# Talking-heads attention and a seven-product MLP on one core: one weight product for all four batches, with the conversion's stores and loads placed anew

## The chip, the cores and the metric

The kernel runs on one core of a Trainium2 chip. The metric is the device time of one execution in microseconds. Three runs of the kernel before gave 1107.64, 1112.34 and 1112.71 us.

## What is computed

Queries, keys, values and mixing weights come in float32, the two MLP weights in float64 (two 32-bit words to a number); inside, each matmul operand is a float32r number, for most operands with a second one that holds the rest. With 4 batches, 12 heads, 448 positions and head size 64:

```python
scores = np.matmul(q, k.transpose(0, 1, 3, 2)) / np.sqrt(64)
scores = np.einsum('bhij,hg->bgij', scores, w_pre)          # mix heads
attn = softmax(scores)
attn = np.einsum('bhij,hg->bgij', attn, w_post)             # mix heads again
x = np.matmul(attn, v).transpose(0, 2, 1, 3).reshape(1792, 768)
h = x @ w_in                                                # 768 x 2048
return (h / (1 + np.exp(-h))) @ w_out                       # 2048 x 768
```

## The kernel before

**Attention.** The scores of 16 tiles (4 batches of 4) are worked on in 180 groups of 10 query rows times 12 heads. For each group TensorE (PE) mixes the heads (`pp`, L317), VectorE (DVE) takes the maximum (`nm`, L323), ScalarE (ACT) the exponential (`e`, L328), GpSimd (POOL) scales the second mixing matrix (`wr`, L336), and PE mixes again (`pa`, L343). In between, the scores of the next tile are made (`pqk`, L277), copied to one of three buffers `st` by ACT (L282) and sent to the group layout `g` by a DMA (L283); the values `po` (L292) of the tile before go through `xb` to `x_dram` (L305). All DMAs are issued by SyncE (SP), in the order in which the program is written: a DMA that waits for its data or its buffer holds up all those behind it.

**Conversion.** `convert` (L38) turns the float64 weights into float32 sums of blocks, in 48 jobs of two parts. A part is a load `cw` (L47, 256 KB), four DVE operations (L82, L88, L89, L63), one of ACT (L86) and a POOL product `cg` (L69); after the second part POOL adds seven block sums (L71 to L74) and a store (L57, 448 KB) puts them into `wi_dram` or `wo_dram`. It is a generator of three pieces to a part; 38 jobs run beside the attention, a part in about two groups, the other 10 in the MLP, three pieces in two steps. A load is issued three parts ahead; with one `cg` buffer the store is issued in the piece right after POOL's last sum.

**MLP.** Each of two units (u = 0, 1) holds two batches. A product of a 2 x 2 block matrix is made from seven block products (`ORDER`, L465), first x by w_in ("i"), then the result by w_out ("o"). A step is one output block of one block product: 9 matmuls of 128x448 in "i" (8 steps to a block product), 24 in "o" (3 steps). The order is u = 0 "i", u = 0 "o", u = 1 "i", u = 1 "o" (L486). For every step the weights are loaded (`wl`, L501), rounded by ACT (`wh`, L513) and the rest is taken by POOL or DVE (`wl`, L525); thus each weight block is loaded and split twice, once for each unit. The operands `op` of a block product are halved by ACT (L549) and DVE (L551) one block product ahead, in one of two sets; `differ` (L553) and `second` (L559, with `t`) make the combined blocks with DVE and POOL. `evacuate` (L718) takes PSUM out after each step. x is read back from `x_dram` in chunks (`load_x`, L468) and added by POOL for unit 0 and by DVE for unit 1.

Of the kernel before, what the change touches and what calls it, by code (L numbers as in the profile page):

```python
# [8 lines left out]
F32 = mybir.dt.float32  # L9
# [28 lines left out]
def convert(nc, pool, ebias, jobs, bufs):  # L38

    parts = [(n, i) for n in range(len(jobs)) for i in (1, 0)]  # L40
    loaded, held = [], []

    def load(k):
        if k < len(parts):
            n, i = parts[k]
            ws = pool.tile([128, 2, 256], I32, name="cw", tag="cw", bufs=4)
            nc.sync.dma_start(out=ws, in_=jobs[n][0][:, i])  # L47
            loaded.append(ws.rearrange("p q (w t) -> p q w t", t=2))
# [5 lines left out]
    def store(most=0):  # L54
        while len(held) > most:
            dst, g = held.pop(0)
            nc.sync.dma_start(out=dst, in_=g)  # L57

    def finish(k, pair, e):
# [6 lines left out]
        if i:  # L66
            finish.g = pool.tile([128, 7, 128], F32, name="cg", tag="cg", bufs=bufs)
        g = finish.g
        nc.gpsimd.tensor_mul(out=g[:, 0:2] if i else g[:, 2:4], in0=m, in1=e.bitcast(F32))  # L69
        if not i:  # L70
            nc.gpsimd.tensor_add(out=g[:, 4], in0=g[:, 0], in1=g[:, 1])  # L71
            nc.gpsimd.tensor_add(
                out=g[:, 5:7], in0=g[:, 0:5:4], in1=g[:, 2:3].to_broadcast([128, 2, 128]))
            nc.gpsimd.tensor_add(out=g[:, 0], in0=g[:, 6], in1=g[:, 3])  # L74
            held.append((jobs[n][1], g))

    before = None
    for k in range(len(parts)):
        pair = loaded.pop(0)
        hi = pair[:, :, :, 1]  # L80
        e = pool.tile([128, 2, 128], I32, name="ce", tag="ce", bufs=2)
# [8 lines left out]
        store(bufs - 1)  # L90
        load(k + 3)
        before = k, pair, e
# [9 lines left out]
def talking_heads_then_silu_mlp(  # L102
# [41 lines left out]
    wi_dram = [dram.tile([128, 7, HC, 128], F32, name=f"wi_dram{f}") for f in range(HF)]  # L144
    wo_dram = [dram.tile([128, 7, HF, 128], F32, name=f"wo_dram{c}") for c in range(HC)]
# [213 lines left out]
    jobs = [(wi_src[:, f, c], wi_dram[f][:, :, c, :]) for f in range(HF) for c in range(HC)]  # L359
    jobs += [(wo_src[:, c, f], wo_dram[c][:, :, f, :]) for c in range(HC) for f in range(HF)]  # L360
    NA = 38
    conv = convert(nc, c_p, ebias, jobs[:NA], 1)
# [56 lines left out]
    for i in range(0, n_last, 10):  # L419
        lighter |= set(sorted(range(i, min(i + 10, n_last)), key=lambda i: weight[i - 1] if i else 0.0)[:10])  # L420
# [45 lines left out]
    xs, gr, ops, box = {}, {}, {}, {}  # L466

    def load_x(u, ls, lag, add):  # L468

        chunks = [(j, l, c) for l in ls for j in range(2) for c in range(HC)]  # L470
        xr = []
        for n in range(len(chunks) + lag):
            if n >= lag:
                r = xr[n - lag]
                add.tensor_add(out=xs[chunks[n - lag]], in0=r[:, 0], in1=r[:, 1])
            if n < len(chunks):
                j, l, c = chunks[n]
                xr.append(box["xr"].tile([128, 2, T], F32, name="xr", tag="xr"))
                for o in range(2):
                    nc.sync.dma_start(  # L480
                        out=xr[n][o * D:(o + 1) * D],
# [4 lines left out]
    steps = [(u, kind, k, a) for u in range(NU) for kind, n in (("i", HF), ("o", HC)) for k in range(7) for a in range(n)]  # L486
    parts, part_of = [], []
    for u, kind, m, a in steps:
        part_of.append(len(parts))
        if kind == "i":  # L490
            parts.append((wi_dram[a][:, ORDER[m]], HC))
        else:
            parts += [(wo_dram[a][:, ORDER[m], h:h + 4], 4) for h in range(0, HF, 4)]
    part_of.append(len(parts))
    raws, ready = {}, {}

    def load_to(i):
        for j in range(load_to.n, min(i, len(parts))):
            w, n = parts[j]
            raws[j] = box["w"].tile([128, 4, 128], F32R, name="wl", tag="wl", bufs=5)  # L500
            nc.sync.dma_start(out=raw(raws[j][:, :n]), in_=w)  # L501
            load_to.n = j + 1

    load_to.n = 0

    turn = {part_of[s] + d for s, x in enumerate(steps) if x[1:] == ("o", 0, 0) for d in range(4)}

    def high_to(i):
        for j in range(high_to.n, min(i, len(parts))):
            high_to.n = j + 1  # L510
            n = parts[j][1]
            wh = box["w"].tile([128, 4, 128], F32R, name="wh", tag="wh", bufs=5)
            nc.scalar.copy(out=wh[:, :n], in_=raw(raws[j][:, :n]))  # L513
            ready[j] = wh, raws.pop(j)

    high_to.n = 0

    def ready_to(i):
        high_to(i)
        for j in range(ready_to.n, min(i, len(parts))):  # L520
            ready_to.n = j + 1
            n = parts[j][1]
            wh, wl = ready[j]
# [3 lines left out]
    ready_to.n = 0  # L527

    def operand(kind, k):

        if kind == "i":
            return [ops[3 * (k % 2) + c] for c in range(HC)]
        return [ops[8 * (1 - k % 2) + c] for c in range(HF)]

    def product(s, p):

        u, kind, k, a = steps[s]
        xs_ = operand(kind, k)
        w = [(ready[j][0][:, c], ready[j][1][:, c]) for j in range(part_of[s], part_of[s + 1]) for c in range(parts[j][1])]
        for n, (x, (wh, wl)) in enumerate(zip(xs_, w)):  # L540
            nc.tensor.matmul(p[:, :T], lhsT=wh, rhs=x[:, 0], start=(n == 0), stop=False)  # L541
            nc.tensor.matmul(p[:, :T], lhsT=wh, rhs=x[:, 1], start=False, stop=False)  # L542
            nc.tensor.matmul(p[:, :T], lhsT=wl, rhs=x[:, 0], start=False, stop=(n == len(xs_) - 1))  # L543
        for j in range(part_of[s], part_of[s + 1]):
            del ready[j]
# [13 lines left out]
    def second(blocks, c, dst):  # L559

        t = box["t"].tile([128, T], F32, name="t2", tag="t2", bufs=4)
        nc.vector.tensor_sub(out=t, in0=blocks[1, 1, c], in1=blocks[0, 0, c])  # L562
        yield
        nc.scalar.copy(out=dst[:, 0], in_=t)
        yield
        nc.gpsimd.tensor_sub(out=blocks[1, 0, c], in0=t, in1=blocks[1, 0, c])  # L566
# [3 lines left out]
    first_step = {(u, kind, k): s for s, (u, kind, k, a) in reversed(list(enumerate(steps)))}  # L570
# [8 lines left out]
    for u in range(NU):  # L579
        for kind, n, blocks in (("i", HF, xs), ("o", HC, gr)):  # L580
            for m in range(7):
                s = first_step[u, kind, m]
                nk = HC if kind == "i" else HF
                if m == 2:
                    todo = [lambda b=blocks, c=c, kind=kind: second(b, c, operand(kind, 2)[c]) for c in range(nk)]
                else:
                    todo = [lambda b=blocks, c=c, kind=kind, m=m: halve(b[(*SOURCE[m], c)], operand(kind, m)[c]) for c in range(nk)]
                if m == 0 and kind == "i":
                    if u:
                        put_at(s - HC, HC, todo)  # L590
                elif m == 0:
                    put_at(s - 2 * HF, 2 * HF - 2, todo)
                else:
                    lag = 3 if (kind, m) == ("i", 2) else 0
                    put_at(s - n + lag, n - lag - (kind == "i"), todo)
# [234 lines left out]
```

## Time and profile before

| | |
|---|---|
| median of three runs | 1112.34 us |
| profiled execution: its time / its span | 1114.52 / 1112.8 us |
| PE, PEld busy | 985.9 us (89%), 792.2 us (71%) |
| DVE, ACT, POOL busy | 778.8 us (70%), 645.0 us (58%), 562.3 us (51%) |
| mean granted TensorE clock | 0.955 |
| DMA queue of SP | 216068 packets, 174.11 MB |

Busy times are unions over an engine's instructions; matmuls overlap in the records, so a busy PE need not be PE at its best pace. Times inside the program are counted from the start of the span. The attention fills the first 623 us, the MLP the rest.

### The profile page before, as it was taken

How to read it: one execution, taken by the hardware profiler on the slowest of the kernel's cores; microseconds unless marked ns; L12 is line 12 of the kernel's file. 1: busy time of each engine (PE TensorE's matmuls, PEld its weight loads, DVE VectorE, ACT ScalarE, POOL GpSimd, SP SyncE). 2: the span in 40 equal slices, each digit the busy share in tenths (PEclk: the TensorE clock that was granted, in tenths of full speed). 3: DMA queues.
4: the chain of work that ended last, by engine and by line, in shares of the span. 5: the costliest groups of instructions: out<-in, count | busy, mean ns of one | idle time of the engine just before them, and what ended most of it. 6: DMA issues, size and time to landing. Idle time of an engine off the chain costs nothing. (4 is left out here: it accounts for less than half of the span.)

```text
span 1112.8 us, 18086 instructions
## 1 busy us (share of the span) xinstructions
PE 985.9 (89%) x5448; PEld 792.2 (71%) x5448; DVE 778.8 (70%) x1751; ACT 645.0 (58%) x1562; POOL 562.3 (51%) x674
## 2 busy tenths in 40 slices
PE   5888999798899988898998878888899999988998
PEld 3456666565676666566777767777699889977897
DVE  2567768766787777488766389887996264869742
ACT  4666666665677766577775444564355453652543
POOL 0354334543344633245414387746965395559752
PEclk8889999988999989899999889999999999999999
DMA  6556756756667666567535756645475433333343
GB/s 169 160 172 173 202 169 195 199 156 174 186 178 215 190 175 172 165 172 199 163 111 146 183 159 193 206 126 146 129 206 145 133 102 106 107 106 84 109 123 96
DMA packets 216164, 175.25 MB, mean 157 GB/s; under 512 B 79524, under 2 KB 205316, under 8 KB 216068
## 3 DMA queue, kind: packets, MB, share of 16 engines
q1 hardware_dynamic: 216068, 174.11, 56.4%
q8 instruction: 44, 0.72, 0.3%
q14 instruction: 52, 0.43, 0.1%
HBM read 96.77 MB, written 38.58 MB: 122 GB/s over the span
## 5 line engine op out<-in xcount | busy, mean ns | idle before, releaser
L543 PE MATMUL ph<-op,wl 128*128 128x448 f32 x672 | 255.1, 380 | 37.6 <-POOL wl L525 29.7
L525 POOL TENSOR_TENSOR wl<-wl,wh 128x384 fp32r<-128x384 f32 (+1 forms) x165 | 211.4, 1292 | 122.5 <-ACT wh L513 115.4
L541 PE MATMUL ph<-op,wh 128*128 128x448 f32 x672 | 253.9, 378 | 2.0 <-ACT wh L513 1.6
L542 PE MATMUL ph<-op,wh 128*128 128x448 f32 x672 | 252.1, 375 | 2.9 <-DVE op L567 2.7
L336 POOL TENSOR_SCALAR wr<-wpost,r 120x120 f32<-120x120 f32 x180 | 85.2, 474 | 308.6 <-DVE r L334 242.5
L343 PE MATMUL pa<-wr,e 120*112 120x120 f32 x1440 | 194.1, 280 | 9.0 <-DVE r L333 7.5
L343 PEld LDWEIGHTS pa<-wr,e 120*112 120x112 f32 x1440 | 168.9, 184 | 36.9 <-issue 20.0
L317 PE MATMUL pp<-g,wpre 120*120 120x448 f32 x360 | 174.9, 570 | 12.1 <-ACT e L328 8.0
L292 PE MATMUL po<-at,v 112*128 112x220 f32 (+1 forms) x768 | 172.5, 352 | 2.6 <-ACT st L282 2.3
L323 DVE TENSOR_REDUCE nm<-pp 120x1 f32<-120x448 f32 x180 | 111.2, 618 | 87.9 <-PE pp L317 86.8
L543 PEld LDWEIGHTS ph<-op,wl 128*128 128x128 f32 x672 | 130.3, 194 | 59.5 <-POOL wl L525 38.3
L513 ACT CAST wh<-wl 128x384 fp32r<-128x384 f32 (+1 forms) x196 | 107.6, 556 | 106.1 <-DMA wl<-wo_dram 54.5
L292 PEld LDWEIGHTS po<-at,v 112*128 112x128 f32 x768 | 115.0, 196 | 71.1 <-issue 53.2
L328 ACT ACTIVATE e<-pp,nm 120x448 f32<-120x448 f32 x180 | 114.7, 637 | 61.0 <-DVE nm L323 60.5
L542 PEld LDWEIGHTS ph<-op,wh 128*128 128x128 f32 x672 | 130.3, 194 | 15.8 <-DVE op L567 4.3
L352 ACT CAST at<-pa 112x480 fp32r<-112x480 f32 x180 | 102.8, 571 | 66.4 <-PE pa L343 65.9
L541 PEld LDWEIGHTS ph<-op,wh 128*128 128x128 f32 x672 | 130.3, 194 | 13.7 <-ACT wh L513 2.2
L282 ACT COPY st<-pqk 110x448 f32<-110x448 f32 (+1 forms) x192 | 98.0, 542 | 69.9 <-DMA g<-st 66.3
L355 DVE TENSOR_TENSOR at<-pa,at 112x480 fp32r<-112x480 f32 x180 | 116.4, 646 | 4.9 <-ACT at L352 4.9
L551 DVE TENSOR_TENSOR op<-g,op 128x448 fp32r<-128x448 f32 x96 | 84.9, 922 | 42.1 <-ACT op L549 42.0
L277 PE MATMUL pqk<-kh,qh 64*110 64x448 f32 (+1 forms) x192 | 65.9, 463 | 47.2 <-ACT st L282 19.0
L69 POOL TENSOR_TENSOR cg<-cw,ce 128x256 f32<-128x256 f32 x96 | 76.4, 796 | 59.2 <-DVE cw L63 20.9
(82 smaller groups left out, 1394.8 us busy)
## 6 DMA issues: line engine op xcount, KB each, us to landing
g<-st SPq DMA_DIRECT2D x144, 192.5 KB
wl<-wi_dram SPq DMA_DIRECT2D x112, 192.0 KB
wl<-wo_dram SPq DMA_DIRECT2D x84, 256.0 KB
cw<-in_moe_w_in SPq DMA_DIRECT2D x48, 256.0 KB
cw<-in_moe_w_out SPq DMA_DIRECT2D x48, 256.0 KB
wi_dram<-cg SPq DMA_DIRECT2D x24, 448.0 KB
wo_dram<-cg SPq DMA_DIRECT2D x24, 448.0 KB
xr<-x_dram SPq DMA_DIRECT2D x48, 224.0 KB
```

The costliest lines, as they stand in the source:

```text
L292: nc.tensor.matmul(po[:, :2 * m].rearrange("p (w t) -> p w t", w=2), lhsT=vs[b, h][:, j].rearrange("p a d -> p (a d)"), rhs=ats[n][:, j, h ...
L317: nc.tensor.matmul(self.p[:GP, :S], lhsT=wpre.rearrange("p i g -> p (i g)"), rhs=gs[self.n][:, self.slot, :], start=True, stop=True)
L323: nc.vector.tensor_reduce(out=self.nm, in_=self.p[:GP, :S], axis=AX.X, op=ALU.max, negate=True)
L328: nc.scalar.activation(out=self.e, in_=self.p[:GP, :S], func=AF.Exp, bias=self.nm, scale=1.0, accum_out=self.s)
L343: nc.tensor.matmul(self.pa[:JT, j * GP:(j + 1) * GP], lhsT=self.e[:, j * JT:(j + 1) * JT], rhs=self.wr, start=True, stop=True)
L352: nc.scalar.copy(out=self.hi, in_=self.src)
L355: nc.vector.tensor_sub(out=self.lo, in0=self.src, in1=raw(self.hi))
L513: nc.scalar.copy(out=wh[:, :n], in_=raw(raws[j][:, :n]))
L525: eng.tensor_sub(out=wl[:, :n], in0=raw(wl[:, :n]), in1=raw(wh[:, :n]))
L541: nc.tensor.matmul(p[:, :T], lhsT=wh, rhs=x[:, 0], start=(n == 0), stop=False)
L542: nc.tensor.matmul(p[:, :T], lhsT=wh, rhs=x[:, 1], start=False, stop=False)
L543: nc.tensor.matmul(p[:, :T], lhsT=wl, rhs=x[:, 0], start=False, stop=(n == len(xs_) - 1))
```

## The change

- The MLP's steps are ordered by block product first and unit second (`steps`): all seven block products of "i" for u = 0 and u = 1 in turn, then those of "o". The weights come in parts of four 128-column blocks, six to a block product and 84 in all, each loaded, rounded and split once (`load_part`, `ready_part`); POOL makes every difference. `load_at` and `high_at` say in which step a part is loaded and made ready; seven buffers (WB) hold the parts.
- Each unit has one set of operands `ops[u]`, rewritten while the other unit's product of the same number runs. `differ` and `second` of both units therefore fall into neighbouring steps.
- Unit 1's x is read during the first block product of "i" and added by POOL.
- In `convert` the store of a job is issued one part after its sums (`store()` at odd k), the load of part k+1 at the start of part k, with three `cw` and two `cg` buffers; the exponent part is made inside `cg`. 34 jobs (NA) run beside the attention, in 8 of every 10 groups; 14 in the MLP, one piece in a step.
- `oT` has two buffers for three, `t` three for four; seven `wl` loads for three are issued in the last tile, and two plus four weight parts are made ready before the MLP.

```diff
     for k in range(len(parts)):
+        if k > 1:
+            load(k + 1)
         pair = loaded.pop(0)
         hi = pair[:, :, :, 1]
-        e = pool.tile([128, 2, 128], I32, name="ce", tag="ce", bufs=2)
+        if k % 2 == 0:
+            g = pool.tile([128, 7, 128], F32, name="cg", tag="cg", bufs=2)
+        else:
+            store()
+        half = g[:, 2 * (k % 2):2 * (k % 2) + 2]
+        e = half.bitcast(I32)
...
-        store(bufs - 1)
-        load(k + 3)
...
-    NA = 38
-    conv = convert(nc, c_p, ebias, jobs[:NA], 1)
+    NA = 34
+    conv = convert(nc, c_p, ebias, jobs[:NA])
...
-        lighter |= set(sorted(range(i, min(i + 10, n_last)), key=lambda i: weight[i - 1] if i else 0.0)[:10])
+        lighter |= set(sorted(range(i, min(i + 10, n_last)), key=lambda i: weight[i - 1] if i else 0.0)[:8])
...
-    steps = [(u, kind, k, a) for u in range(NU) for kind, n in (("i", HF), ("o", HC)) for k in range(7) for a in range(n)]
+    steps = [(kind, k, u, a) for kind, n in (("i", HF), ("o", HC)) for k in range(7) for u in range(NU) for a in range(n)]
+    NP = HF * HC // 4
+    parts = [(src, ORDER[k], p) for src in (wi_dram, wo_dram) for k in range(7) for p in range(NP)]
...
+    WB = NP + 1
+    for j in range(WB, len(parts)):
...
+        s = step_of[kind0, m0, NU - 1, (4 * p0 + 3) // n] + 1
+        s = max(s, step_of[kind, m, 0, 0] - (10 if kind == "i" or m == 0 else 3))
+        load_at[s].append(j)
+        high_at[s + (3 if s < step_of["o", 0, 0, 0] - 2 else 1)].append(j)
...
-            eng = nc.vector if j % 2 and (2 <= j < 7 * HF or j in turn) else nc.gpsimd
-            eng.tensor_sub(out=wl[:, :n], in0=raw(wl[:, :n]), in1=raw(wh[:, :n]))
+        nc.gpsimd.tensor_sub(out=wl, in0=raw(wl), in1=raw(wh))
...
+                if kind == "i" and u and not m:
+                    put_at(s - n + 3, n - 3, todo)
+                elif m or u:
+                    put_at(s - n, n - (kind == "i"), todo)
+                elif kind == "o":
+                    put_at(s - HF, HF - 1, todo)
                 if m == 1:
-                    lag = n if kind == "i" else 0
-                    put_at(s - n + lag, n // 2 if lag else n, [lambda b=blocks, c=c: differ(b, c) for c in range(nk)])
+                    put_at(s, n, [lambda b=blocks, c=c, u=u: differ(b[u], c) for c in range(nk)])
...
         if s > 2:
             next(conv, None)
-            if s % 2:
-                next(conv, None)
```

SP in the attention, around a store of the conversion (`cg`), before; `st` to `g` are the scores, `xb` the values:

```order
L283 DMA g<-st 10x11x448 x2
L57 DMA wi_dram_72<-cg 896x1x128
L47 DMA cw<-in_moe_w_in 128x2x256
L305 DMA x_dram_67<-xb 128x2x110
L283 DMA g<-st 10x11x448 x2
```

The same place after the change:

```order
L284 DMA g<-st 10x11x448 x2
L47 DMA cw<-in_moe_w_in 128x2x256
L206 DMA kn<-in_k 112x4x64 x2
L306 DMA x_dram_67<-xb 128x2x110
L243 DMA qn<-in_q 120x6x64
L47 DMA cw<-in_moe_w_in 128x2x256
L57 DMA wi_dram<-cg 896x1x128
```

The store went from just ahead of the scores' next DMAs to behind the load of the following part.

SP at the start of the MLP after the change; `xr` are chunks of x for unit 1, `cw` the MLP's first conversion loads:

```order
L306 DMA x_dram_70<-xb 128x2x110 x7
L481 DMA xr_7540<-x_dram_69 64x2x448 x2
L481 DMA xr_7541<-x_dram_69 64x2x448 x2
L481 DMA xr_7540<-x_dram_69 64x2x448 x2
L481 DMA xr_7541<-x_dram_69 64x2x448 x2
L47 DMA cw<-in_moe_w_out 128x2x256 x3
```

DVE there, after the change (`op` are unit 1's first operands, L86 and L92, L93 the conversion):

```order
L539 TENSOR_TENSOR op_8041<-x_8035,op_8041 128x448
L86 TENSOR_SCALAR cg<-cw 128x256
L539 TENSOR_TENSOR op_8042<-x_8036,op_8042 128x448
L92 SCALAR_TENSOR_TENSOR cg<-cw,cg 128x256
L93 TENSOR_SCALAR cw<-cw 128x256
L539 TENSOR_TENSOR op_8043<-x_8037,op_8043 128x448
```

Ahead of the three `cw` loads SP now has four chunks on two buffers, and a conversion operation stands between the first and the second of unit 1's operands.

DVE in the second product, block products 1 and 2, before (unit 1; `g` the blocks, L555 `differ`, L562 and L567 `second`):

```order
L555 TENSOR_TENSOR g_8213<-g_8221,g_8213 128x448
L562 TENSOR_TENSOR t_11720<-g_8230,g_8206 128x448
L562 TENSOR_TENSOR t_11723<-g_8231,g_8207 128x448
L567 TENSOR_TENSOR op_8198<-t_11720,op_8198 128x448
```

The same place after the change (L543 `differ` of unit 1, L550 and L555 `second` of unit 0):

```order
L543 TENSOR_TENSOR g_8083<-g_8075,g_8083 128x448
L550 TENSOR_TENSOR t_10458<-g_8060,g_8052 128x448
L550 TENSOR_TENSOR t_10463<-g_8061,g_8053 128x448
L550 TENSOR_TENSOR t_10465<-g_8062,g_8054 128x448
L555 TENSOR_TENSOR op_7537<-t_10458,op_7537 128x448
L732 TENSOR_TENSOR oT<-ph,x_8035 128x448
L555 TENSOR_TENSOR op_7538<-t_10463,op_7538 128x448
```

One unit's `differ` and the other's `second` now stand in the same three steps.

## Rows read from the trace of the kernel before

**Rows 1.** Windows: start:end, length; busy us (count) PE PEld DVE ACT POOL; clock, DMA, GB/s.

```profile
45.00:603.00 558.00, 497.64 (x3093) 365.41 (x3093) 406.10 (x1209) 374.95 (x1010) 233.44 (x387) 0.96 0.63 175
...
623.30:756.70 133.40, 111.00 (x488) 95.81 (x488) 107.93 (x196) 67.47 (x143) 84.38 (x90) 0.94 0.63 178
756.70:878.30 121.60, 111.74 (x546) 100.33 (x544) 96.39 (x100) 55.02 (x105) 84.49 (x57) 0.97 0.56 151
878.30:985.20 106.90, 105.86 (x515) 95.07 (x513) 62.61 (x90) 60.60 (x126) 66.65 (x61) 1.00 0.41 113
985.20:1106.50 121.30, 112.12 (x543) 101.30 (x543) 79.72 (x86) 53.05 (x102) 80.11 (x55) 0.96 0.37 102
940.60:970.35 29.75, 29.75 (x145) 27.03 (x144) 21.48 (x32) 19.28 (x40) 15.55 (x16) 1.00 0.38 106
```

**Rows 2.** Tile ph, what its engine sat idle for: us, times.

```profile
  POOL wl L525: 68.0, 44
...
  DVE wl L525: 18.0, 12
```

**Rows 3.** Groups of DVE by line, 623 to 745 us: count, busy us, mean ns, idle before.

```profile
L88 DVE SCALAR_TENSOR_TENSOR ce<-cw,ce 128x256 int32<-128x256 int32 x20 | 13.9, 696 | 5.3 <-ACT ce L86 5.3
L525 DVE TENSOR_TENSOR wl<-wl,wh 128x384 fp32r<-128x384 f32 x23 | 13.7, 594 | 3.5 <-ACT wh L513 3.5
L89 DVE TENSOR_SCALAR cw<-cw 128x256 int32<-128x256 int32 x20 | 13.1, 653 | 0.7
...
L82 DVE TENSOR_SCALAR ce<-cw 128x256 int32<-128x256 int32 x20 | 8.4, 419 | 5.7 <-DMA cw<-in_moe_w_out 5.7
L63 DVE SCALAR_TENSOR_TENSOR cw<-cw 128x256 f32<-128x256 uint32 x20 | 8.3, 415 | 0.0
...
L745 DVE TENSOR_TENSOR g<-g,ph 128x448 f32<-128x448 f32 x8 | 4.9, 616 | 1.1 <-PE ph L543 1.0
```

**Rows 4.** Timeline of the MLP's first steps: start us, us, what [idle before <- releaser].

```profile
625.10 2.54 SPq L480 DMA_DIRECT2D xr<-x_dram  x4
...
627.80 1.50 SPq L47 DMA_DIRECT2D cw<-in_moe_w_out  x3
...
629.82 1.13 POOL L475 TENSOR_TENSOR x<-xr 128x448 f32<-128x448 f32 x1 [3.07 <-DMA xr<-x_dram]
...
632.89 0.45 DVE L82 TENSOR_SCALAR ce<-cw 128x256 int32<-128x256 int32 x1 [5.66 <-DMA cw<-in_moe_w_out]
...
633.86 0.74 PE L543 MATMUL ph<-op,wl 128*128 128x448 f32 x1 [4.46 <-DVE wl L525]
```

**Rows 5.** Timeline of DVE, second product of unit 1.

```profile
990.73 1.16 DVE L551 TENSOR_TENSOR op<-g,op 128x448 fp32r<-128x448 f32 x2 [2.48 <-ACT op L549]
...
992.35 0.61 DVE L551 TENSOR_TENSOR op<-g,op 128x448 fp32r<-128x448 f32 x1
...
1006.10 3.33 DVE L555 TENSOR_TENSOR g<-g,g 128x448 f32<-128x448 f32 x2
...
1031.05 3.06 DVE L567 TENSOR_TENSOR op<-t,op 128x448 fp32r<-128x448 f32 x2
```

**Rows 6.** Timeline of POOL, the same stretch.

```profile
985.28 1.29 POOL L525 TENSOR_TENSOR wl<-wl,wh 128x512 fp32r<-128x512 f32 x1 [2.32 <-ACT wh L513]
...
1008.91 1.54 POOL L557 TENSOR_TENSOR g<-g,g 128x448 f32<-128x448 f32 x1
1010.41 3.31 POOL L525 TENSOR_TENSOR wl<-wl,wh 128x512 fp32r<-128x512 f32 x2
```

**Rows 7.** Waits of SP's queue, 45 to 590 us: us in total, times, longest.

```profile
SPq L283 <- ACT st L282: 69.9, 51, 5.0
SPq L57 <- POOL wr L336: 62.7, 26, 6.5
```

**Rows 8.** Waits of the engines, 45 to 590 us.

```profile
ACT st L282 <- DMA g<-st: 57.5, 36, 4.2
...
PE pqk L277 <- ACT st L282: 19.0, 13, 3.9
```

**Rows 9.** Groups of DVE by line, 45 to 590 us.

```profile
L323 DVE TENSOR_REDUCE nm<-pp 120x1 f32<-120x448 f32 x166 | 102.5, 618 | 74.6 <-PE pp L317 73.6
```

**Rows 10.** The chain that ended last, 884 to 889 us.

```profile
884.92 3.51 DMA wl<-wi_dram
```

More of the change, by code (lines that the diff above doesn't have):

```diff
@@ L52, in convert, with store, finish @@
     yield
-    def store(most=0):
-        while len(held) > most:
-            dst, g = held.pop(0)
+    def store():
+        while made:
+            dst, g = made.pop(0)
             nc.sync.dma_start(out=dst, in_=g)
-    def finish(k, pair, e):
+    def finish(k, pair, g, e):
         n, i = parts[k]
@@ L65, in finish @@
             op0=ALU.mult, op1=ALU.add if i else ALU.subtract)
[L66 to L69, printed above, removed]
+        nc.gpsimd.tensor_mul(out=e, in0=m, in1=e)
         if not i:
@@ L487, in talking_heads_then_silu_mlp @@
[L487 to L494, printed above, removed]
-    raws, ready = {}, {}
[L497 to L502, printed above, removed]
@@ new lines, in talking_heads_then_silu_mlp, with load_part, ready_part @@
+    high_at[3].append(NP)
+    def load_part(j):
+        src, k, p = parts[j]
+        if src is wo_dram:
+            for _ in conv:
+                pass
+        raws[j] = box["w"].tile([128, 4, 128], F32R, name="wl", tag="wl", bufs=WB)
+        nc.sync.dma_start(out=raw(raws[j]), in_=src[:, k, 4 * p:4 * p + 4])
+    def ready_part(j):
+        wl = raws.pop(j)
+        wh = box["w"].tile([128, 4, 128], F32R, name="wh", tag="wh", bufs=WB)
+        nc.scalar.copy(out=wh, in_=raw(wl))
+        nc.gpsimd.tensor_sub(out=wl, in0=raw(wl), in1=raw(wh))
+        ready[j] = wh, wl
@@ L541, in product @@
+    def product(s, p):
+        kind, k, u, a = steps[s]
+        nk = HC if kind == "i" else HF
+        for n in range(nk):
+            wh, wl = (x[:, (a * nk + n) % 4] for x in ready[part_of(kind, k, a * nk + n)])
+            x = ops[u][n]
             nc.tensor.matmul(p[:, :T], lhsT=wh, rhs=x[:, 0], start=(n == 0), stop=False)
             nc.tensor.matmul(p[:, :T], lhsT=wh, rhs=x[:, 1], start=False, stop=False)
-            nc.tensor.matmul(p[:, :T], lhsT=wl, rhs=x[:, 0], start=False, stop=(n == len(xs_) - 1))
@@ L544, in product @@
-        for j in range(part_of[s], part_of[s + 1]):
-            del ready[j]
+            nc.tensor.matmul(p[:, :T], lhsT=wl, rhs=x[:, 0], start=False, stop=(n == nk - 1))
     def halve(src, dst):
@@ L788, in talking_heads_then_silu_mlp @@
         each = -(-len(todo) // rounds)
-        for _ in range(rounds):
+        last = a == (HF if kind == "i" else HC) - 1
+        while todo or rounds > 0 or last and active:
+            rounds -= 1
             active.extend(todo[:each])
```

187 lines of the change are left out of this document (85 added, 102 removed).

## The prediction

> **What bounds the kernel now.** I read the windows by stage first: in each row the reader should compare PE's count and busy time with the length. The quiet row at the end of the group gives PE's pace where nothing holds it: 16 steps of 9 matmuls in 29.75 us, so 0.2066 us a matmul [rows 1]. At that pace unit 0's first product from step 2 on (54 steps, 486 matmuls) needs 100.4 us and took 133.4, a loss of 33.0. Unit 1's (504 matmuls, 104.1 us) took 106.9, a loss of 2.8. The two second products (504 each) took 121.6 and 121.3, a loss of 17.5 and 17.2, with the output transposes in it, which stay. Next I asked what PE stood idle for at the tile of the MLP's results: 68.0 us in 44 waits for weight remainders made by POOL, 18.0 in 12 for those made by DVE [rows 2]. So the MLP is held by the splitting of weights, most of all where the conversion shares the engines. In the attention PE was busy 497.6 of 558.0 us at a mean clock of 0.96 [rows 1]; 19.0 us of its idle time ended with ACT's copy of scores, and ACT itself waited 57.5 us for earlier scores' DMAs [rows 8]. SP, which issues them in order, stood 62.7 us in 26 waits at the conversion's store, whose sums POOL had not made [rows 7].
>
> **First product: 18 us gained.** The change halves the weight work: 196 loads, roundings and differences become 84, of 512 columns where most had 384, and DVE makes none. What takes over is DVE's total. Before, in 8 steps (14.9 us) of unit 0, DVE had 4 conversion parts of 0.696 + 0.653 + 0.419 + 0.415 = 2.18 us, 8 evacuations of 0.616, 4 weight differences of 0.594 and 3 operand halves of about 0.7 [rows 3]: 8.7 + 4.9 + 2.4 + 2.1 = 18.1, or 3.2 too much, which is why unit 0 lost and unit 1, with no conversion, hardly did. After it, 16 steps (29.75 us) hold 5.3 parts, 16 evacuations and 6 halves: 11.6 + 9.9 + 4.2 = 25.7, which fits, for block products 3 and 4. Block product 1 is the exception: beside evacuations and conversion it has 3 halves, both units' `differ` (6) and unit 0's `second` (6). At 0.61 us where POOL is quiet and 1.67 where POOL runs beside it (3.33 for two) [rows 5], about 1.0 on the mean, that is 11.6 + 9.9 + 15 = 36.5, 7 too much. Four PSUM banks let PE run some steps ahead, so I charge 7 us for it, with block product 2, which only just fits, in that.
>
> The start has a wait of its own. In the present kernel two chunks of x are issued from 625.10 on, the first is added at 629.82; the conversion's loads go out at 627.80, DVE's first conversion operation waits until 632.89, and PE loses 4.46 us behind it [rows 4]. After the change SP has four chunks ahead of those loads, on two buffers, so the third waits for the first to be added. By these rows: first add done 7.6 us after the start of step 2 (630.95 less 623.3), third chunk then out, loads out near 10.3, landed near 15.4. DVE's conversion operation stands before the second operand of unit 1, and ACT's conversion step before the third. PE wants them in step 8, 6 steps or 11.2 us in, and gets them near 17. So 5 to 6 us, and about 2 for the lower clock after it, my estimate from unit 0's mean of 0.94 where the quiet row has 1.00 [rows 1]: 7.5. It takes the place of the present 4.46 and what followed. With 3 for the rest, the loss is 7.5 + 7 + 3 = 17.5 against 33.0 + 2.8 = 35.8. Bounds: 8 us gained if block product 1 costs all the DVE excess twice (both units), 28 if the banks hide it.
>
> **Second product: 8 us gained.** With weights off the path, the work behind `differ` and `second` decides. Now: one unit's chain on DVE ran from 990.73 to 1034.1, 43.4 us [rows 5], for 32 operations on two operands in SBUF and 3 evacuations on DVE, and 28 on POOL (8, 8 and 12 weight differences). DVE alone takes 0.61 [rows 5], POOL alone 1.29 for 512 columns; with both running, one of each takes 1.5 (1008.91 to 1010.41) [rows 6] to 1.67. At 1.55 the sum is 28 x 1.55 + 7 x 0.6 = 47.6, so the measured chain is 0.91 of it. Its last operand was wanted 6 steps of 4.96 us and 4.3 more after 985.2, at 1019.3: 14.8 late, the bulk of 17.2. Both units together: 29.6. After: both units' `differ` and `second` follow on each other. From the first step of block product 1 there are 56 such operations and 9 evacuations on DVE, and 16 + 16 + 7 on POOL: (39 x 1.55 + 26 x 0.6) x 0.91 = 69.2. The last is wanted 9 steps and 4.3 us on, at 48.9: 20.3 late, against 29.6, so 9, and I take 8, since the single operand set can start nothing early. The weight parts have 10 us from load to use (two steps) for 3.5 us of load [rows 10], ACT's rounding and POOL's 1.3 to 1.7 [rows 6], and are late only with the chain. Unit 1's 12 additions of x leave DVE for POOL in the first product, already counted.
>
> **A rule that speaks against this.** Two-operand additions on DVE slow from 0.61 to 1.67 us when POOL runs [rows 5]. The Trainium skill (GPSIMD Engine Reference, Key points) says that GpSimd shares its SBUF interfaces with VectorE and contends with DVE instructions that have two SBUF inputs; the trace agrees. Taken strictly, as turns without overlap, a pair would cost the sum of the two alone, which is the third rival below.
>
> **Attention: 10 us gained.** Four jobs leave, but DVE and POOL are not full there. What counts is SP: the store moves behind the next part's load, so POOL's sums are long made, and the scores' DMAs no longer queue behind it. I take half of PE's 19.0 us [rows 8], as ACT also waits for scores with no store in front. Upper bound: all 19.0 and part of the clock, whose 0.96 over 558 us is 22 us: 25. Lower bound 0, since stores and loads still share the DMA engines. A weight part in the last tile is 256 KB instead of 192, and seven are issued together: 0 to 2 us, within the rounding.
>
> **Sum.** 18 + 8 + 10 = 36 us against the profiled execution's 1114.5; its span is 1112.8, and it stands 2.2 above the median of 1112.3. From the median: **1076 us**.
>
> **Rivals.** First, SP gives more: all PE waits for score copies go (25), block product 1 hides in the banks (24): 1112 - 25 - 24 - 8 = 1055. For it: the 62.7 us [rows 7]; against: ACT's waits also where only scores were issued.
>
> Second, the same sum is lost again: DVE's excess spreads over the first product (108 of 133 us are DVE's already [rows 1]) and the waits only change their name: 1108 to 1112. Against it: unit 1 without conversion loses 2.8.
>
> Third, DVE and POOL take strict turns in the second product: 32 pairs at 0.61 + 1.13 (1.29 for 448 of 512 columns), 7 at 0.61 + 1.29 and 26 x 0.6 make 84.6, or 36 late instead of 20: 1076 + 16 = 1092. Against it: pairs at 1.5 [rows 6].
>
> Fourth, **slower**: a conversion load is now issued one part ahead, not three, and DVE's first operation on it stands in DVE's queue before `nm` of a following group. Two groups take 2 x 545 / 166 = 6.6 us [rows 9], a load 3.5 [rows 10] to 5.1 [rows 4] and SP's own delay. It decides if loads land 7.1 us or more after their part began: at 0.55 us late on each of 66 parts the 36 us are gone, at 1 us it is 1076 + 66 = 1142. Against it: DVE's idle time there hides some, and 3.5 leaves 3 us.
>
> **Chances.** Forecast 0.54, first rival 0.20, second 0.06, third 0.14, fourth 0.06. The range takes the first rival whole and the third with 12 more for its bounds: 1050 to 1104; outside are the second, the fourth, and some of the tails. About 0.5% (5.6 us) is what a measurement here can tell from no change: faster 0.88, same 0.06, slower 0.06.
>
> **What would show it.** Right: 84 splits, no weight difference on DVE; PE's idle time for POOL's weights below 25 us; one stall of 5 us or so near step 8; stalls at block products 1 and 2 of "o" with `second` as releaser, some 20 us; SP's waits at the store near zero. Wrong: a first conversion operation that waits for `cw` in most parts of the attention, or evacuations as releaser through all of the first product.

## The result, and the profile after

The changed kernel takes **1081.73 us** (median of 4 runs, 1077.76 to 1085.65) where the kernel before took 1112.53 on the same chip (4 runs, 1107.64 to 1117.17): a ratio of 0.9724, interval 0.9668 to 0.9779. The forecast was 1076, within 1050 to 1104. A run more than 1.5% above the fastest of its kernel is left out of medians and ratios; that is one run, 1073.96 us of the kernel of four moves below. The profiled execution took 1082.58 us, its span is 1080.9 (before 1114.5 and 1112.8).

For the comparison both spans are cut at three events: the first weight load (`wl`) in the last attention tile, the first matmul of step 2 of the MLP, and the first matmul of the second product. Windows of the kernel after (columns as in [rows 1]):

```profile
45.00:579.70 534.70, 488.27 (x3083) 359.72 (x3080) 392.95 (x1173) 369.56 (x999) 216.76 (x367) 0.98 0.63 175
579.70:610.00 30.30, 19.98 (x122) 17.89 (x121) 9.74 (x31) 10.94 (x34) 16.45 (x16) 0.89 0.77 209
610.00:839.40 229.40, 211.87 (x993) 189.12 (x993) 173.74 (x284) 100.82 (x198) 134.82 (x137) 0.96 0.46 133
839.40:1074.60 235.20, 222.99 (x1095) 200.90 (x1094) 144.25 (x179) 86.71 (x170) 100.93 (x71) 0.96 0.22 61
```

In the kernel before the first weight load is at 603.1, step 2 at 623.4; its products are those of [rows 1], the two units added.

| stretch | before | after | difference | forecast |
|---|---|---|---|---|
| attention, up to the first weight load | 603.1 | 579.7 | -23.4 | -10 |
| hand-over, from there to step 2 | 20.3 | 30.3 | +10.0 | 0 (priced 0 to 2) |
| first products | 240.3 | 229.4 | -10.9 | -18 |
| second products | 242.9 | 235.2 | -7.7 | -8 |
| last transposes and stores | 6.3 | 6.3 | 0 | 0 |
| sum | | | -32.0 | -36 |

So the sum is close, but its parts are not: the attention gave more than twice what was forecast, the hand-over took 10 us back, and the first product gave 7 less. The MLP, for which the weights are now taken once, gave 18.6 us in its two products and 8.6 with the hand-over; most of the 32 us comes from the attention.

The attention's 23.4 us is the difference of two profiled executions. Six runs below have the same program up to the first weight load; in their profiles it stands at 579.7 to 586.0 us, so the gain is 17 to 23 us, and the hand-over of those kernels that load twelve chunks of x as the changed one does (below) takes 30.3 to 33.7.

The waits of SP's queue and of the engines, 45 to 590 us, which answer to [rows 7] and [rows 8]:

```profile
SPq L284 <- ACT st L283: 99.0, 60, 4.6
SPq L306 <- DVE xb L304: 89.4, 51, 4.7
...
SPq L57 <- POOL wr L337: 10.9, 5, 5.0
```

```profile
ACT st L283 <- DMA g<-st: 41.4, 43, 3.0
...
PE pqk L278 <- ACT st L283: 11.5, 11, 2.8
```

SP's wait at the store fell from 62.7 us to 10.9. ACT waits 16 us less for the scores' DMAs, and PE 7.5 less for ACT's copies. SP now stands idle longer for scores and results themselves, that is, for work that it is early for. PE's idle time in the attention fell from 60.4 us (558.0 less 497.64) to 46.4, and its busy time by 9.4, which is the granted clock: 0.96 before, 0.98 after.

Idle time at the tile of the MLP's results (the view of [rows 2]), and the one group that now makes weight remainders. The view adds up every engine that writes or reads the tile: lines with a PE releaser are evacuations that waited for matmuls, and in the other lines TensorE's two rows, matmuls (PE) and weight loads (PEld), are summed, so that most stalls stand in them twice:

```profile
  PE ph L533: 57.6, 48
  DVE op L539: 14.7, 5
  ACT g L729: 13.7, 8
  PE ptt L756: 11.9, 3
  DVE g L732: 8.1, 13
  DVE x L555: 7.5, 3
  ACT xr L552: 6.3, 2
```

```profile
L521 POOL TENSOR_TENSOR wl<-wl,wh 128x512 fp32r<-128x512 f32 x84 | 116.4, 1396 | 133.5 <-ACT wh L520 133.3
```

The 68.0 and 18.0 us for weight remainders are gone (2.0 are left, 0.4 of it PE's own); 84 splits are left, none on DVE. In their place stand operands made by DVE (`op`, `x`), evacuations (`g`) and, at `x` and `xr`, the operands of `second`.

Where the first product loses is read by step: at the pace of [rows 1] its 990 matmuls take 204.5 us, so 24.9 are lost. Taking each step's length less nine matmuls gives three places: 7.5 at the first two steps of unit 1; 8.9 where block product 0 passes into 1; 10.3 in the rest of block products 1 and 2 (4.2 and 6.1). Together that is 26.7, with 0.3 more in block product 0; block products 3 to 6, 29.2 us each, are quicker than the pace by 2.2 in all. The first two places in the timeline of the kernel after:

```profile
621.73 1.60 SPq L47 DMA_DIRECT2D cw<-in_moe_w_out  x3
...
626.91 0.29 DVE L86 TENSOR_SCALAR cg<-cw 128x256 int32<-128x256 int32 x1 [7.54 <-DMA cw<-in_moe_w_out]
...
627.79 0.74 PE L532 MATMUL ph<-op,wh 128*128 128x448 f32 x1 [5.25 <-DVE op L539]
```

```profile
632.91 8.82 SPq L481 DMA_DIRECT2D xr<-x_dram  x8
641.78 0.58 SPq L515 DMA_DIRECT2D wl<-wi_dram  x1
```

```profile
645.33 0.62 ACT L520 CAST wh<-wl 128x512 fp32r<-128x512 f32 x1 [7.69 <-DMA wl<-wi_dram]
645.86 0.53 ACT L729 COPY g<-ph 128x448 f32<-128x448 f32 x1
```

```profile
646.44 0.47 PE L531 MATMUL ph<-op,wh 128*128 128x448 f32 x1 [2.39 <-ACT g L729]
...
651.25 0.47 PE L531 MATMUL ph<-op,wh 128*128 128x448 f32 x1 [2.72 <-ACT g L729]
```

The first is the stall that was forecast: conversion loads out 11.7 us after step 2, PE held 5.25 us. The second was not forecast: SP spends 8.8 us on eight DMAs of x, as it stands parked for POOL to free one of two buffers, and the weight part behind them goes out late. ACT, which must round that part, waits 7.69 us for it, and the evacuation at 645.86, which PE needs, stands behind ACT's wait. PE loses 2.39 us there and 2.72 behind ACT's next wait for a weight part (3.76 us); most of the rest of the 8.9 is the granted clock, 0.70 between 650 and 655 us.

### The profile page after: what moved, and what is told of

Same layout as the page of the kernel before. It is cut to its first block, busy times and chain, and to the rows that moved or that the text cites. A ratio compares the mean times of both kernels' runs of the same rounds, so it can differ in the third digit from the quotient of the medians.

```text
span 1080.9 us, 17390 instructions
## 1 busy us (share of the span) xinstructions
PE 976.7 (90%) x5448; PEld 787.8 (73%) x5448; DVE 737.8 (68%) x1708; ACT 593.9 (55%) x1450; POOL 474.5 (44%) x605
## 4 chain that ended last, share of the span: by engine, by line
PE 43%; DVE 21%; DMA 20%; ACT 8%; issue 5%; SPq 2%; POOL 2%; ACTq 0%; POOLq 0%; DVEq 0%
DMA g<-st 13%; PE ph L532 10%; PE ph L531 10%; PE ph L533 10%; PE pa L344 5%; DVE nm L324 3%; PE pp L318 3%; DMA xr<-x_dram 3%; PE pqk L278 3%; ACT st L283 3%; DVE at L356 3%; DVE t L550 2%; ACT e L329 2%; DVE cg L92 1%; PE po L293 1%
## 5 line engine op out<-in xcount | busy, mean ns | idle before, releaser
L344 PEld LDWEIGHTS pa<-wr,e 120*112 120x112 f32 x1440 | 165.6, 181 | 48.0 <-issue 24.7
L531 PE MATMUL ph<-op,wh 128*128 128x448 f32 x483 | 183.5, 380 | 11.6 <-ACT g L729 6.0
L532 PE MATMUL ph<-op,wh 128*128 128x448 f32 x483 | 180.8, 374 | 8.1 <-DVE op L539 6.8
L533 PE MATMUL ph<-op,wl 128*128 128x448 f32 x483 | 180.0, 373 | 0.1
L318 PE MATMUL pp<-g,wpre 120*120 120x448 f32 x360 | 171.9, 562 | 7.8 <-DMA g<-st 4.8
L521 POOL TENSOR_TENSOR wl<-wl,wh 128x512 fp32r<-128x512 f32 x84 | 116.4, 1396 | 133.5 <-ACT wh L520 133.3
L531 PEld LDWEIGHTS ph<-op,wh 128*128 128x128 f32 x483 | 93.0, 193 | 24.4 <-ACT g L729 7.7
L532 PEld LDWEIGHTS ph<-op,wh 128*128 128x128 f32 x483 | 93.2, 193 | 17.3 <-DVE op L539 7.9
L533 PEld LDWEIGHTS ph<-op,wl 128*128 128x128 f32 x483 | 93.1, 193 | 8.7 <-POOL wl L521 0.8
L66 POOL TENSOR_TENSOR cg<-cw,cg 128x256 f32<-128x256 f32 x96 | 71.5, 745 | 42.7 <-DVE cw L63 42.7
L304 DVE TENSOR_TENSOR xb<-po,xb 128x110 f32<-128x110 f32 (+1 forms) x192 | 50.2, 268 | 51.8 <-ACT xb L301 51.5
L520 ACT CAST wh<-wl 128x512 fp32r<-128x512 f32 x84 | 51.0, 617 | 42.0 <-DMA wl<-wi_dram 22.4
```

What stands on the lines that cost most here:

```text
L318: nc.tensor.matmul(self.p[:GP, :S], lhsT=wpre.rearrange("p i g -> p (i g)"), rhs=gs[self.n][:, self.slot, :], start=True, stop=True)
L344: nc.tensor.matmul(self.pa[:JT, j * GP:(j + 1) * GP], lhsT=self.e[:, j * JT:(j + 1) * JT], rhs=self.wr, start=True, stop=True)
L521: nc.gpsimd.tensor_sub(out=wl, in0=raw(wl), in1=raw(wh))
```

## The experiments

**The attention: whose gain is it?** First, the old kernel with nothing but the new conversion routine (`convert` exchanged whole; 38 jobs and the choice of groups as before).

> The kernel before, with nothing of the change but its conversion routine (store one half job later, loads one part ahead, 38 jobs and all groups as before). Theory (the gain of the attention is SP no longer parked at the store): the first weight load of the last tile falls from 603 us to about 582, SP's wait at the store for POOL's sums from 62.7 us to below 15, and the time to 1088 to 1096 us; the MLP stays within 4 us of before. Rival (the attention gained because four jobs and every fifth group of conversion left it): 1105 to 1112 us, the first weight load past 598.

Measured 1099.39 us, ratio 0.9859 (0.9795 to 0.9923). Windows with the same three cuts, and SP's waits at the store up to 570 us:

```profile
45.00:580.30 535.30, 485.99 (x3097) 357.69 (x3096) 404.81 (x1209) 375.79 (x1011) 230.72 (x388) 0.98 0.66 183
580.30:601.90 21.60, 17.17 (x115) 16.65 (x113) 9.37 (x29) 9.41 (x29) 8.21 (x9) 0.84 0.49 135
601.90:1085.00 483.10, 436.20 (x2086) 387.71 (x2085) 341.74 (x473) 236.06 (x472) 313.42 (x262) 0.98 0.50 138
```

```profile
SPq L57 <- POOL wr L338: 8.2, 8, 2.4
```

The first weight load moves to 580.3, where the changed kernel has it, though no job left the attention; the MLP, 483.10 us, is as long as before to a tenth. The median is 3 us beyond the range expected; the kernel before itself took 1117.35 in these runs. The profile fell on the fastest of four runs (1092.96 to 1104.69): by the ratio this run gains 1.4%, 16 us, of the changed kernel's 31, by the profiles 23. Second, the changed kernel with the store put back behind the sums (`now` is true for the attention's conversion alone):

```diff
             made.append((jobs[n][1], g))
+            if now:
+                store()
```

> The changed kernel with the attention's stores issued at once behind POOL's sums again; the MLP's conversion is left as the change has it. Theory (store): SP waits over 50 us at the store, the first weight load of the last tile goes from 579.7 us to 597 or later, time 1098 to 1106 us. Rival (fewer jobs, or the third buffer and load order): 1079 to 1086 us.

Measured 1138.56 us, ratio 1.0208 (1.015 to 1.0267): slower than the kernel before. Its first window, and SP's wait at the store:

```profile
45.00:636.60 591.60, 511.90 (x3079) 374.72 (x3078) 390.68 (x1172) 372.24 (x1000) 216.59 (x368) 0.93 0.57 159
```

```profile
SPq L57 <- POOL wr L339: 122.6, 29, 8.1
```

The direction was expected, the size not: SP is parked for 122.6 us, as this store stands earlier than that of the kernel before, and the attention grows by 57 us: PE is idle for 33 us more (79.7 for 46.4), and nearly the same matmuls keep it busy for 24 us more, at a granted clock of 0.93 instead of 0.98. The MLP keeps its length. Two runs in opposite directions and an untouched MLP: the gain of the attention is the conversion's place in SP's queue, and not the jobs that left. The second `cg` buffer does not bring the gain by itself, as this run has it too; a late store with one buffer was not tried.

**The hand-over: chunks of x or weight loads?** The last tile now loads twelve chunks of x through two buffers, where six were loaded before, and seven weight parts at once for three. One run takes six chunks out of it, the other spreads the weight loads.

```diff
-            x_next = load_x(0, ((0, 0), (1, 0), (0, 1), (1, 1)), 2)
+            x_next = load_x(0, ((0, 0), (1, 0)), 2)
...
```

> The changed kernel, but only the six chunks of x that the first two block products of unit 0 need are loaded in the last attention tile; the other six follow in the MLP, behind the first three of unit 1. Theory (the ten us lost between the first weight load and step 2 come from twelve chunks on two buffers, whose waits hold SP and with it the stores of results): this stretch falls from 30.3 us to 22 to 25, time 1074 to 1078 us, unless the late chunks hold block product 1 of unit 0, which would give back up to 5. Rival (the burst of seven weight loads): 1080 to 1084, stretch within 2 of 30.3.

```diff
-                for j in range(WB):
+                for j in range(3):
                     load_part(j)
...
         if h % 3 == 0:
             ready_part(len(ready))
+            load_part(3 + h // 3)
```

> The changed kernel, but three weight parts are loaded at the fifth group of the last tile and four between its last heads, instead of seven at once. Theory (chunks of x): stretch from first weight load to step 2 falls by 0 to 2 us from 30.3, time 1079 to 1083. Rival (burst of seven loads, 1.8 MB before the stores of results): the stretch falls to 20 to 24 and the time to 1072 to 1077.

Measured 1081.59 us (0.9697, 0.9641 to 0.9753) with six chunks, 1085.39 (0.9738, 0.9689 to 0.9786) with three loads. From the first weight load to step 2, six chunks and then three loads:

```profile
578.80:601.80 23.00, 17.11 (x132) 15.80 (x132) 10.79 (x33) 11.40 (x34) 12.80 (x12) 1.00 0.55 156
```

```profile
579.60:613.30 33.70, 21.83 (x133) 20.57 (x133) 10.19 (x31) 10.97 (x33) 16.51 (x16) 0.75 0.72 184
```

Six chunks give 23.0; with the weight loads spread out the stretch is 3.4 us longer and not shorter, so their burst is not the cause. In the eight profiles of kernels with the new MLP and twelve chunks this stretch took 30.3 to 33.7, in the four with six chunks 22.8 to 24.5. So the chunks make 7 of the 10 us; the other 3 against the kernel before (20.3) stay open. How it works is seen in the changed kernel: SP stands 10.0 us for POOL's additions of x between 570 and 612 us (2.8 with six chunks), the stores of results queue behind, and ACT waits for them:

```profile
591.27 0.25 ACT L301 COPY xb<-po 128x110 f32<-128x110 f32 x1 [4.26 <-DMA x_dram<-xb]
598.47 0.25 ACT L301 COPY xb<-po 128x110 f32<-128x110 f32 x1 [5.88 <-DMA x_dram<-xb]
```

In time it is not to be told from the changed kernel: the late chunks come due in block product 1, which grew from 40.4 to 48.0 us, and the first product from 229.4 to 232.2.

**The first product: three places, three causes?** One run begins the conversion at step 17 instead of 3 (`if s > 16`), one at step 41 with three of its steps in two product steps, one gives x in the MLP six buffers instead of two.

> The changed kernel with the MLP's conversion begun at step 17, after block product 0, instead of step 3. Theory (the stall at the first step of unit 1 is DVE and ACT standing at a conversion part whose loads lie behind chunks of x; the losses of block products 0 to 2 are DVE's and ACT's sum with conversion in it): the stall of 7 us at that step is gone and block product 0 falls from 56.7 us to 47 to 50; block products 1 and 2 lose as much as now or up to 5 more, the others stay at 29.2; first product 222 to 226 us against 229.3. Rival (the additions of x on POOL hold unit 1's first operands, conversion or not): block product 0 stays at 55 or more.

> The changed kernel with the MLP's conversion begun at step 41 and three steps of it in two product steps, so that it ends where it did. Theory (sum of DVE and ACT): block products 0 to 2 lose under 8 us in all instead of 26, block products 3 to 5 lose 0 to 6 as they hold 1.4 times the conversion; first product 206 to 216 us against 229.3, time 1063 to 1072 us. Rival (the loss of block products 1 and 2 is the operands' own chain, differ and second of both units with POOL beside DVE, conversion or not): first product 220 or more.

> The changed kernel, but unit 1's chunks of x land in six buffers in turn instead of two in the MLP (four of them tiles that are first written in block product 4), with three chunks issued ahead; conversion as in the change. Theory now (what holds ACT, and behind it the evacuations, at the end of block product 0 is a weight part that SP issues late, since it stands parked at chunks whose buffer POOL has not freed): ACT's wait for weight parts between steps 2 and 30 falls from 14.3 us to under 4, the stall at the first step of unit 1 from 7 to under 3, and the first product from 229.3 to 212 to 218 us; time 1066 to 1072. Rival (the sum of DVE and ACT with the conversion in it holds block product 0 too): first product 225 or more with PE waiting for DVE instead.

Measured: 1076.17 us (0.9653, 0.9602 to 0.9704), 1080.88 (0.9697, 0.9661 to 0.9734), 1079.83 (0.9701, 0.967 to 0.9731). The length of each block product, from the first matmul of one to that of the next (block product 0 from step 2 on), and of the whole first product:

| kernel | 0 | 1 | 2 | 3 | 4 | 5 | 6 | all |
|---|---|---|---|---|---|---|---|---|
| changed kernel | 36.4 | 40.4 | 35.8 | 29.2 | 29.2 | 29.2 | 29.2 | 229.4 |
| six chunks in the last tile | 31.6 | 48.0 | 35.9 | 29.1 | 29.2 | 29.2 | 29.2 | 232.2 |
| conversion from step 17 | 34.5 | 33.4 | 35.7 | 29.2 | 29.2 | 29.2 | 29.2 | 220.4 |
| conversion from step 41 | 33.4 | 31.7 | 29.8 | 29.7 | 30.3 | 36.7 | 32.8 | 224.5 |
| six buffers | 37.6 | 32.5 | 35.8 | 29.2 | 29.1 | 29.2 | 29.2 | 222.6 |

Without conversion in block product 0 the first stall (7.5) is gone, and the passage to block product 1 still loses 8.6, with ACT waiting 12.15 us for a weight part: the conversion had nothing to do with that. I had expected block product 0 itself to fall to the length of a quiet one, and missed that place. With conversion from step 41 block products 1 and 2 fall by 14.7 us together, and 5 and 6 give 11.1 of it back, with PE waiting 8.2 us for evacuations on DVE: the conversion costs the same work wherever it is put, and only block products 3 and 4 have room for more of it. With six buffers SP's waits at the chunks of x for POOL go from 12.9 us to 0.7 between 610 and 660, ACT's wait from 7.69 to 1.61, and block product 1 from 40.4 to 32.5:

```profile
645.24 0.62 ACT L520 CAST wh<-wl 128x512 fp32r<-128x512 f32 x1 [1.61 <-DMA wl<-wi_dram]
```

But its first stall did not shrink, as I expected; it grew from 7.5 to 10.8, with DVE waiting 10.9 us for the conversion's loads: more chunks were under way ahead of them; and the first product fell to 222.6, not to 212 to 218. In whole time none of the three runs (two executions for the first, four for the others) is clear of the changed kernel, whose interval is 0.9668 to 0.9779. So the three places have three causes, shown one by one: conversion loads behind x, a weight part behind x, and the conversion's work in block products 1 and 2; that this work tells through the sum of DVE and ACT is argued from the forecast's count, not shown.

**The second product: late or full?** The forecast took 20.3 us of lateness from a chain that starts too late for its length. So `differ` was begun three, then six steps earlier.

```diff
-                    put_at(s, n, [lambda b=blocks, c=c, u=u: differ(b[u], c) for c in range(nk)])
+                    put_at(s - n if kind == "o" else s, n, [lambda b=blocks, c=c, u=u: differ(b[u], c) for c in range(nk)])
```

> The changed kernel, but in the second product each unit's differences of blocks (differ) begin one unit's steps earlier, three steps, 14.6 us. Theory (the stall of 21 us at block product 2 is the chain of differ and second of both units on DVE, late as forecast): it starts 14.6 us earlier and DVE has room there, so block product 2 falls from 50.7 to 34 to 39 us and the second product from 235.2 to 219 to 223; time 1066 to 1070. Rival (DVE and POOL are slowed by each other wherever this work stands, so the work and not its start sets the loss): second product 230 or more, with stalls in block products 0 and 1.

> The changed kernel, but differ of the second product begins six steps (29.2 us) earlier, in block product 0. Theory A (the chain is bound by the work on DVE and POOL, and POOL's turn with the weight parts is what made three steps earlier bring only 5.4 us): 16 differences on POOL now lie in block product 0, which has room for 8 of them, so about 10 us more: second product 217 to 223 us. Theory B (each two-operand pair slows the other wherever it stands): 227 to 231, with stalls in block products 0 and 1 for weight parts.

Measured 1081.61 us (0.97, 0.9664 to 0.9737) and 1084.14 (0.9731, 0.9696 to 0.9766); second product 229.8 and 230.6 us for 235.2. My theory falls in both: 14.6 and 29.2 us of start brought 5.4 and 4.6, and 230.6 lies where theory B has it. Part of that may be spread: in six other profiles with the changed kernel's second product it took 232.6 to 235.2. The stall only parts in two, block product 1 going from 30.9 to 37 and 2 from 50.7 to 40. Windows of the second run, block product 0 of unit 0, of unit 1, and the stalled start of block product 1:

```profile
847.80:862.40 14.60, 14.60 (x73) 13.55 (x73) 13.50 (x15) 6.09 (x13) 10.74 (x9) 1.00 0.07 20
862.40:877.00 14.60, 14.60 (x73) 13.54 (x72) 14.60 (x15) 8.13 (x16) 11.28 (x8) 1.00 0.33 90
877.00:891.80 14.80, 11.92 (x45) 10.46 (x44) 14.80 (x12) 3.85 (x8) 14.24 (x10) 0.77 0.00 0
```

In the second window DVE is busy for all of 14.6 us with 15 operations that take 0.61 alone, and POOL beside it. I read this as a DVE that is full because POOL is working; the last run below tests it.

**Versions from the parts.** The first puts together six chunks in the last tile, conversion from step 41 and `differ` three steps earlier; the second has six chunks, six buffers, conversion from step 39 (one and a half steps of it up to step 79) and `differ` six steps earlier.

> The changed kernel with six chunks of x in the last tile, conversion begun at step 41 at one and a half steps, and differ of the second product three steps earlier. If the three losses are separate: 7 us at the hand-over, 15 to 22 in the first product, 14 in the second, so 1040 to 1048 us. If the late chunks of x hold block product 1 whatever DVE does: first product 218 or more and 1052 or more.

> The changed kernel with six buffers for x in the MLP, six chunks of x in the last tile, conversion from step 39 (three steps of it in two product steps up to step 79), and differ six steps earlier. If the losses are separate causes as the single runs show: hand-over 23 us, first product 206 to 212, second 218 to 226; time 1044 to 1054 us. If the start of the MLP is still held by the late chunks of x: first product 220 or more, time 1060 or more.

Measured 1075.48 us (0.9647, 0.9599 to 0.9696), where the late chunks hold block product 1 at 42.6 us, and 1060.21 (0.9531, 0.9498 to 0.9564), with a first product of 219.0 and a second of 229.8. Both missed their ranges (1040 to 1048, 1044 to 1054): the losses were not simply separate, and only the hand-over came as expected (22.8 us). The third adds to the second one:

```diff
-        nc.gpsimd.tensor_sub(out=blocks[0, 1, c], in0=blocks[1, 1, c], in1=blocks[0, 1, c])
+        eng.tensor_sub(out=blocks[0, 1, c], in0=blocks[1, 1, c], in1=blocks[0, 1, c])
...
-        nc.gpsimd.tensor_sub(out=blocks[1, 0, c], in0=t, in1=blocks[1, 0, c])
+        eng.tensor_sub(out=blocks[1, 0, c], in0=t, in1=blocks[1, 0, c])
...
+        eng = nc.gpsimd if kind == "i" else nc.vector
...
-        next(x_next, None)
+        if s not in (13, 15, 17, 19):
+            next(x_next, None)
```

> The kernel of the four moves (last run) with two more: in the second product the second operations of differ and second go to DVE, where their first ones are, so that POOL makes only weight differences there; and after the eleventh step one chunk of x follows in two steps instead of in each. Theory of the second product (one pair of differences, one on DVE and one on POOL at the same time, takes about 1.5 us and both on DVE 2 x 0.55): DVE's share of block products 0 to 2 falls though it does 32 operations more, the stalls there go from 16 us to 2 to 8, the second product from 229.8 to 214 to 222. Rival (DVE is full and each operation moved to it adds its time): 232 or more. Theory of the first product (weight parts are late there since chunks of x fill the DMA engines): the wait of 12 us for a weight part falls below 7 and the first product from 219.0 to 211 to 216. Rival: 218 or more. Time 1040 to 1054 us if both hold, 1062 or more if neither.

Measured **1055.33 us**, ratio 0.9471 (0.9436 to 0.9506): faster than both kernels. The second product fell from 229.8 to 218.2, its stalls in block products 1 and 2 from 16 to 4 (38.6 and 38.2 us, then 31.2 and 33.8, where 30.9 and 29.75 are the lengths without a stall). Groups of DVE in its first three block products, the kernel of four moves first, then this one (L545 was on POOL before; the second operation of `second`, L553, also went to DVE and is not shown):

```profile
L550 DVE TENSOR_TENSOR t<-g,g 128x448 f32<-128x448 f32 x16 | 18.3, 1171 | 0.0
L543 DVE TENSOR_TENSOR g<-g,g 128x448 f32<-128x448 f32 x16 | 16.4, 1055 | 0.0
```

```profile
L545 DVE TENSOR_TENSOR g<-g,g 128x448 f32<-128x448 f32 x16 | 12.5, 803 | 0.1
L550 DVE TENSOR_TENSOR t<-g,g 128x448 f32<-128x448 f32 x16 | 11.5, 720 | 0.0
L543 DVE TENSOR_TENSOR g<-g,g 128x448 f32<-128x448 f32 x16 | 10.7, 686 | 0.0
```

The same 32 operations (L543, L550) take 22.2 us for 34.7. Over the whole second product DVE is busy 138.77 us with 213 operations, where it was 146.88 with 181 (the kernel of four moves, then this one):

```profile
827.40:1057.30 229.90, 220.48 (x1095) 200.11 (x1095) 146.88 (x181) 88.94 (x175) 105.83 (x73) 0.98 0.22 63
```

```profile
829.90:1048.10 218.20, 216.20 (x1095) 197.46 (x1094) 138.77 (x213) 89.10 (x175) 66.29 (x41) 1.00 0.24 66
```

The first product's part of the expectation failed: 219.3 us, and ACT still waits 12.1 us for a weight part. It is now issued in time, but lands 7.7 us later (634.49 to 642.19) instead of 3.5 (641.78 to 645.33 in the changed kernel), with the DMA engines full in the record (the last column but one):

```profile
623.00:630.00 7.00, 7.00 (x36) 6.49 (x35) 2.12 (x2) 3.40 (x7) 3.54 (x4) 1.00 1.07 230
630.00:637.00 7.00, 6.34 (x32) 5.54 (x30) 1.58 (x2) 0.09 (x1) 4.11 (x4) 1.00 1.07 233
637.00:644.00 7.00, 0.71 (x2) 0.67 (x3) 0.00 (x0) 1.05 (x2) 2.24 (x2) 0.79 1.07 247
```

I take it that holding chunks back from step 13 on came too late; that the full DMA engines make the wait is argued, not shown, as holding the chunks back earlier was not tried.

## Why the prediction was right, and where it was not

**The start stall** was forecast at 7.5 us and lost 7.5, at the place and for the reason given. **DVE's sum** in block products 1 and 2 was charged 7, nearly all of it in block product 1, and lost 10.3, of which 6.1 in block product 2, which was to fit; in the run with conversion after them these 10.3 are gone, so they are the conversion's share. What failed in the first product is "3 for the rest": the passage from block product 0 to 1 alone lost 8.9. I had let the conversion's loads queue behind x in SP's queue, but not the weight parts, which stand behind the same chunks; and ACT, that rounds them, evacuates too.

One row was misread: the 68.0 and 18.0 us of [rows 2] are not PE's idle time, but that of matmuls and of weight loads added. PE's own was 37.3 us:

```profile
PE ph L543 <- POOL wl L525: 29.7, 21, 3.4
PE ph L543 <- DVE wl L525: 7.6, 5, 4.5
```

That the MLP was held by weight remainders stands, and no term of the sum rests on the two numbers, as the terms were made from the windows.

**The second product** came out at 7.7 gained for 8, with 21 us of stalls for 20.3, all in block product 2:

```profile
899.50:950.20 50.70, 38.48 (x155) 31.25 (x154) 48.27 (x46) 19.51 (x37) 41.84 (x28) 0.80 0.19 52
```

PE is idle for 12.2 of the 21; the other 8.7 are matmuls at a granted clock of 0.80, of which the forecast's chain says nothing. The price was right, as it was made from pairs at 1.55 us under contention. What the words made of it, a chain that is late, was not: starting it 29.2 us earlier gave 4.6, taking POOL out of it as well 11.6 more. Taking POOL out without the earlier start was not tried, so how much of the 11.6 needs both is open. The Trainium skill (SBUF — State Buffer, SBUF: two separate sides) says that of a DVE instruction with two SBUF inputs and a GpSimd one that reads SBUF, the first to start has the shared ports for its whole length and the other waits. By that, as an estimate, a pair would take the 0.54 from one DVE operation to the next and POOL's 1.13 [rows 4], 1.67; pairs took 1.5, a little less than strict turns, and the third rival (36 us late) did not come. Two operations on DVE alone take 2 x 0.54, as in the last run, where POOL stands still from 885.8 to 890.9 us (each lasts 0.62, and one starts every 0.54):

```profile
889.00 0.62 DVE L550 TENSOR_TENSOR t<-g,g 128x448 f32<-128x448 f32 x1
889.54 0.62 DVE L555 TENSOR_TENSOR x<-t,x 128x448 fp32r<-128x448 f32 x1
```

**The attention** was sized from the wrong row. Half of PE's 19.0 us at score copies was close for that wait (7.5 less), but the rest of the 23.4 lies in other waits of PE (6.5) and in the clock (9.4), and I had put the clock only into the upper bound. The upper bound of 25 was nearly reached in this profile, so the first rival's half on SP came true in size, but not in its account: PE's waits for score copies fell by 7.5, not by all 19.0. Its other half, 24 in the banks, did not come.

**The last tile** was the step left out. "0 to 2 us, within the rounding" priced the weight loads, which indeed cost nothing; the six further chunks of x on two buffers, part of the same edit, were not priced at all; the run without them shows that they cost 7 of the 10. Nothing of the slower rival appeared: up to 570 us the first conversion operation waited for its load once, 0.5 us:

```profile
DVE cg L86 <- DMA cw<-in_moe_w_in: 0.5, 1, 0.5
```

The errors, 13 one way and 17 the other, cancelled to 4: that the time came out so near is luck, though the mechanisms of the start, of DVE's sum and of the second product's price were seen.

## What to carry to other kernels

A DMA queue that issues in order is a resource to be costed like an engine: for every transfer with a wait in front of it, ask which transfers stand behind, and give it more buffers or a later place; then look again, as six buffers here ended one wait (7.69 to 1.61 us) and lengthened another (7.5 to 10.8). When an engine is full, look at the mean time of its operations before moving them away: operations that are slow only because a neighbour works beside them can be got back by giving the engine more of the work. Where a stall only moves when its work starts earlier, as in the second product here, suspect a full engine, and not a late start.

## What the runs showed of the hardware that was not expected

Thirty-two operations more on DVE lowered DVE's own busy time by 8 us, as those that it had before ran up to 1.6 times as fast once POOL's share had gone (`second`'s 1171 to 720 ns on the mean, `differ`'s 1055 to 686). And one store moved ahead of its place parked the issuing queue for 122.6 us and made the whole kernel 57 us slower, with the granted clock of the attention at 0.93 instead of 0.98: PE's gaps cost time twice, 33 us as idle time and 24 in slower matmuls.
